# Wider sums of exponentials, a query transpose on VectorE, and one transfer on another queue in a clustered-attention and feed-forward kernel

## The chip, the cores and the metric

The kernel runs on one core of a Trainium2 chip. The metric is the device time of one launch in microseconds (us), the median of several runs. The engines of a core run their own instruction streams in order and meet at semaphores: PE (TensorE) multiplies, DVE (VectorE) and ACT (ScalarE) work on elements, POOL (GpSimd) here mostly issues transfers, SP (SyncE) issues transfers only.

## What is computed

Attention within clusters, for 4 batches of 8 heads with 768 positions of 64 features, and then a layer norm and a two-layer network on each position:

```python
q_assign = argmax(einsum('bhsd,hcd->bhsc', q_n, c_n))     # q_n, k_n, c_n: q, k, centroids at unit length
k_assign = argmax(einsum('bhsd,hcd->bhsc', k_n, c_n))     # 16 centroids per head
mask = q_assign[:, :, :, None] == k_assign[:, :, None, :]
scores = where(mask, q @ k.T / sqrt(64), -1e9)
attn = exp(scores - max);  attn = attn / (sum(attn) + 1e-9)
x = (attn @ v) laid out as (batch, 768, 512)
xn = (x - mean) / sqrt(var + 1e-6) * g_ln
out = x + relu(xn @ w_ch1) @ w_ch2                        # w_ch1 512x2048, w_ch2 2048x512
```

All inputs are 4-byte floats but the two weight matrices, which come as 8-byte floats and are turned into 4-byte floats on the chip.

## The kernel before

**Pairs, slots, steps.** Two heads are handled together, so that they fill 128 partitions; there are 16 such pairs, n = 0 to 15. A pair is cut in two slots (halves of 384 queries, `g`), a slot in six steps of 128 keys (`c`). A step has three parts in `scores`: two bf16 matmuls that put the cluster mask into a PSUM tile (three such tiles exist), two 4-byte matmuls that add q·k (L407), and one exponential of 128x768 elements on ACT (L402) into a tile `e`, of which there are eight. `weigh` multiplies `e` by v (L419) and, on DVE, adds it to the running sum of exponentials `es` (L433 for the first two, L436 for each later one), so that a slot has five adds of 768 columns. `finish` divides by those sums for an earlier pair: part 0 is a matmul with ones (`den`, L456), part 1 a reciprocal (L471) and transfers that spread it, part 2 a product (L489, L493), part 3 a transpose and a store (L501, L504).

**Preparing the next pair.** During pair n the kernel prepares pair n+1. `prep_transpose` turns k and q so that the features lie on partitions. It has two ways. If the load wrote 32x32 blocks in the right places (`load_blocks`, L86, runs of 128 bytes), one DVE transpose of 128x768 completes the job (L281). Otherwise the load is a plain one (L113), PE does six transposes into PSUM (L286), and ACT copies them out (L291). The set `blocks` holds which: k for all pairs from 1 on, q only for pair 1 and pairs 8 to 15. Then come the similarities to the centroids (`prep_sims`, PE), their transposes (`prep_turn`, PE), the nearest centroid (`prep_route`, DVE, L338 and L340) and the mask (`prep_onehot`, `prep_mask`, PE and ACT).

**Weights.** The 8-byte weights come in 32 chunks of 128x512. `load_weight` fetches one (L237, 512 KB, issued by SP) into the tile `raw`. `split_weight` (L246, L249, L252) reads the upper words of `raw`, `join_weight` (L261, L265, L266) reads its lower words last of all and sends the sum on by a transfer. During attention one such tile exists, `bufs=limit[1]` with

```python
    limit = [NWC, 1]
```

so the load of the next chunk can start only when L266 of the last one has ended. `convert` gives a chunk to both slots of pairs 0 to 6 and to the first slot of pairs 7 to 14, 22 chunks in all; the other ten are converted during the first batch's network.

**Order.** Inside attention the order of PE, DVE, ACT and POOL is the order in which the code is written (`manual_schedule`); SP is placed by the scheduler. In each slot the code writes: the transposes of pair n+1 (first slot only), six `scores`, preparation, six `weigh` with their adds, `finish` parts 1, 2, 3 (second slot), split, join, the next `load_weight`, and in the first slot `load(n+1, "v")`, `prep_turn` and `prep_route`.

**After attention.** The network works through four batches in seven-product block form (`product`, L774; `second_product`, L867).

Of the kernel before, what the change touches and what calls it, by code (L numbers as in the profile page):

```python
# [19 lines left out]
def kernel(  # L20
# [49 lines left out]
    def ps(name, dt=F32, n=512):  # L70
# [4 lines left out]

    TWICE = 7

    blocks = {
        (n, name) for n in range(1, len(pairs)) for name in ("qk" if n == 1 or n > TWICE else "k")
    }  # L80

    def load_blocks(n, name):
        b, pr = pairs[n]
# [10 lines left out]
    def load(n, names):  # L94
        if n >= len(pairs):
            return
        b, pr = pairs[n]
        for name in names:

            if (n, name) in blocks:  # L100
                load_blocks(n, name)
                continue
            shape = [P, 2, NT, D] if name == "v" else [P, NT, 2, D]
            t = loads.tile(
                shape, F32, tag=name, name=f"{name}_sb", bufs=2 if name == "v" else 1
            )

            parts = 1 if n or name == "v" else NHALF
            for g in range(parts):
                cs = slice(g * NT // parts, (g + 1) * NT // parts)  # L110
                for j in range(2):
                    queue = nc.scalar if parts > 1 and j else nc.sync
                    queue.dma_start(  # L113
                        out=t[:, j] if name == "v" else t[:, cs, j, :],
                        in_={"q": q, "k": k, "v": v}[name][b, 2 * pr + j].rearrange(
                            "(p c) d -> p c d", p=P
                        )[:, cs, :],
                    )
            loaded[n][name] = t
# [1 line left out]
    load(0, "q")  # L121

    c_sb = const.tile([H * NCL, D], F32, name="c_sb")
    nc.gpsimd.dma_start(out=c_sb, in_=centroids.rearrange("h c d -> (h c) d"))
    load(0, "k")

    ident = const.tile([P, P], F32, name="ident")
# [1 line left out]
    identb = const.tile([P, P], BF16, name="identb")  # L129
    nc.gpsimd.tensor_copy(identb, ident)  # L130

    once = attn.tile([P, 2, HC], F32, tag="e", name="once", bufs=8)
    zeros = once[:, 0, : P // 2].bitcast(BF16)
    nc.vector.memset(zeros, 0.0)
    ones = const.tile([P, Q], F32, name="ones")
# [135 lines left out]

    prepared = {n: {} for n in range(len(pairs))}

    def prep_transpose(n, side, halves=range(NHALF)):
        src = loaded[n]["qk"[side]]
        if 0 in halves:
            prepared[n][side] = heads.tile([P, S], F32, tag=f"t{side}", name=f"t{side}")
        t_sb = prepared[n][side]
        if (n, "qk"[side]) in blocks:
            if 0 in halves:  # L280
                nc.vector.transpose(t_sb, src)  # L281
            return
        if n:
            t = ps_s.tile([P, 2, 512], F32, tag="s", name="qk_ps")
            for c in range(NT):
                nc.tensor.transpose(  # L286
                    t[:, c // TH, c % TH * P : (c % TH + 1) * P],
                    src[:, c, :, :].rearrange("p h d -> p (h d)"),
                    ident,
                )  # L290
            nc.scalar.copy(t_sb.rearrange("p (g c) -> p g c", g=NHALF), t[:, :, :HC])  # L291
            return
        for g in halves:
            t = ps_s.tile([P, 2, 512], F32, tag="s", name="qk_ps")[:, 0]
            for c in range(TH):
                nc.tensor.transpose(
                    t[:, c * P : (c + 1) * P],
                    src[:, g * TH + c, :, :].rearrange("p h d -> p (h d)"),
                    ident,
                )  # L300
            if side == 0 or g == 1:
                nc.scalar.copy(t_sb[:, g * HC : (g + 1) * HC], t[:, :HC])
            else:
                nc.vector.tensor_copy(t_sb[:, g * HC : (g + 1) * HC], t[:, :HC])
# [86 lines left out]
    def scores(i, first="mask", parts=("mask", "qk", "exp")):  # L391
        n, g, c = steps[i]
        st = prepared[n]
        if parts[0] == first:
            st["s", i] = ps_s.tile([P, 2, 512], F32, tag="s", name="s_ps")
        s = st["s", i]
        keys, cols = slice(c * P, (c + 1) * P), slice(g * HC, (g + 1) * HC)
        rows = [slice(j * D, (j + 1) * D) for j in range(2)]
        for part in parts:
            if part == "exp":  # L400
                e = attn.tile([P, 2, HC], F32, tag="e", name="e", bufs=8)
                nc.scalar.activation(e, s[:, :, :HC], AF.Exp, scale=SCALE)  # L402
                soft[i] = e
                continue
            for j in range(2):
                of_keys, of_queries = st["m"][j] if part == "mask" else [st[i][rows[j]] for i in (1, 0)]
                nc.tensor.matmul(  # L407
                    s[:, j, :HC], of_keys[:, keys], of_queries[:, cols],
                    start=part == first, stop=part != first, skip_group_check=True,
                )  # L410

    def weigh(i):
        n, g, c = steps[i]
        e = soft[i]
        if c == 0:
            accs[n, g] = ps_a.tile([P, 512], F32, tag="a", name="a_ps")
        acc = accs[n, g]
        for j in range(2):
            nc.tensor.matmul(  # L419
                acc[j * D : (j + 1) * D, :HC],  # L420
                loaded[n]["v"][:, j, c, :],
                e[:, j, :],
                start=(c == 0),
                stop=(c == NT - 1),
            )

        if c == 1:
            if n + 1 < len(pairs):
                es = last.tile([P, 2, HC], F32, tag="es", name="es", bufs=3)
            else:  # L430
                es = xpool.tile([P, 2, HC], F32, tag="row", name="es", bufs=2)
            sums[n, g] = es
            nc.vector.tensor_tensor(es, soft.pop(i - 1), soft.pop(i), ALU.add)  # L433
        elif c > 1:
            es = sums[n, g]
            nc.vector.tensor_tensor(es, es, soft.pop(i), ALU.add)  # L436
        if c == NT - 1:
            if g == 0:
                if n + 1 < len(pairs):
                    xs[n] = last.tile([P, S], F32, tag="x", name="x", bufs=3)  # L440
                else:

                    late["all"] = xpool.tile([P, 3, S], F32, tag="sums", name="late", bufs=2)
                    xs[n] = late["all"][:, 0]
            nc.scalar.copy(xs[n][:, g * HC : (g + 1) * HC], accs.pop((n, g))[:, :HC])  # L445

# [229 lines left out]
    with tc.manual_schedule(engines=order | {mybir.EngineType.Pool}):  # L678
        for u in range(len(pairs) * slots):
            n, slot = divmod(u, slots)  # L680
            nxt = n + 1 < len(pairs)
            own = range(GROUP * u, GROUP * (u + 1))
            if slot == 0 and not nxt:
                finish(n - 1, 0)
            if slot == 0 and nxt:
                for side in (1, 0):
                    if (n + 1, "qk"[side]) in blocks:
                        prep_transpose(n + 1, side)
                        load(n + 2, "qk"[side])
            for i in own:  # L690
                if i >= AHEAD:
                    scores(i)
            if slot == 0:
                if n and nxt:
                    finish(n - 1, 0)
                if nxt:
                    prep_sims(n + 1)
            elif nxt:
                prep_onehot(n + 1)
                prep_mask(n + 1, 0)  # L700
                prep_mask(n + 1, 1)
                if n + 2 < len(pairs) and (n + 2, "q") not in blocks:
                    prep_transpose(n + 2, 0)
                    load(n + 3, "q")
            for job in extra.pop((n, f"between {slot}"), ()):
                job()
            for i in own:
                weigh(i)
            if slot and nxt:
                if n:  # L710
                    finish(n - 1, 1)
                if n > 1:
                    finish(n - 2, 2)
                    finish(n - 2, 3)
            if (n, slot) in convert:
                m = convert[n, slot]
                split_weight(m)
                join_weight(m)
                load_weight(m + 1)
            if slot == 0:  # L720
                load(n + 1, "v")
                if nxt:
                    prep_turn(n + 1)
                    prep_route(n + 1)
                else:
                    for part in (2, 3):
                        finish(n - 2, part)
                    finish(n - 1, 1)
            elif not nxt:
                for part in (2, 3):  # L730
                    finish(n - 1, part)
            for job in extra.pop((n, slot), ()):
                job()
# [472 lines left out]
```

## Time and profile before

| | |
|---|---|
| time, median of 3 runs | 933.51 us (930.01 to 934.81) |
| span of the profiled execution | 929.1 us |
| busy, share of the span: PE, DVE, ACT, POOL | 99%, 66%, 38%, 8% |
| attention, pairs 0 to 15 | about the first 343 us |
| DVE busy in attention, for example 110 to 160 us | 46.87 of 50 us |
| the same in the last 289 us | 120.45 of 289 us |

The page of a profile gives for each engine the time in which it worked, then groups of equal instructions with count and mean duration, then the transfers. The trace behind it can be asked for instructions in order of time (the timeline), for waits, and for busy time in stretches. Starts of consecutive instructions are what counts for a rate: the durations shown overlap a little, or leave a short gap where the next one needs the result. The whole-run share of an engine hides stages: DVE is at 66% over the run, but at 94% in parts of attention.

### The profile page before, as it was taken

What the parts mean: (1) busy time and instruction counts of PE and PEld (TensorE: products, weight loads), DVE (VectorE), ACT (ScalarE), POOL (GpSimd) and SP (SyncE); (2) the same over time, 40 slices, a digit from 0 to 9 for tenths busy, and PEclk for the clock granted to TensorE, in tenths of its full rate; (3) what the DMA queues carried; (4) which work ended last, traced back from release to release, by engine and by line L of the source; (5) the groups of instructions that cost most, each with busy time, mean ns of one, the idle gap of its engine ahead of it and who ended that gap; (6) DMA issues with size and microseconds to landing.
All of it is one profiled execution on the core that took longest, in us unless ns stands there. A gap on an engine that the chain in (4) does not pass through costs nothing.

```text
span 929.1 us, 12604 instructions
## 1 busy us (share of the span) xinstructions
PE 918.7 (99%) x4670; PEld 589.1 (63%) x4670; DVE 614.6 (66%) x1104; ACT 349.8 (38%) x551; POOL 78.3 (8%) x146
## 2 busy tenths in 40 slices
PE   8999999999999999999999999999999999999997
PEld 5444444444444445568886558886557887556886
DVE  4988999999899978889772436472346372434331
ACT  4677777767777653330003331002331001332000
POOL 2121222211211112110000000000000000000000
PEclk9999999999999999999999999999999999999999
DMA  7576888999888455645530002120002021000011
GB/s 153 128 162 125 183 177 166 210 185 166 175 175 162 100 119 142 159 91 170 176 112 8 1 0 94 55 74 17 1 0 86 18 96 40 0 1 6 30 46 37
DMA packets 177061, 89.35 MB, mean 96 GB/s; under 512 B 144096, under 2 KB 160592, under 8 KB 176992
## 3 DMA queue, kind: packets, MB, share of 16 engines
q1 hardware_dynamic: 167648, 73.06, 32.8%
q0 software_dynamic: 7744, 15.02, 8.1%
q8 instruction: 39, 0.64, 0.3%
q10 hardware_dynamic: 1600, 0.39, 0.2%
q14 instruction: 30, 0.25, 0.1%
HBM read 62.52 MB, written 17.52 MB: 86 GB/s over the span
## 4 chain that ended last, share of the span: by engine, by line
PE 92%; DVE 3%; DMA 3%; issue 1%; SPq 1%; ACT 0%; DVEq 0%; ACTq 0%
PE x_ps L867 18%; PE x_ps L774 18%; PE s_ps L407 13%; PE a_ps L419 12%; PE z_ps L867 9%; PE z_ps L774 9%; PE y_ps L867 4%; PE y_ps L774 4%; PE den_ps L456 1%; DMA v_sb<-in_v_dram 1%; PE sim_ps L313 1%; DVE es L436 1%; DMA raw<-in_moe_w_ch_dram 1%; PE simT_ps L329 1%; PE oh_ps L355 1%
## 5 line engine op out<-in xcount | busy, mean ns | idle before, releaser
L402 ACT ACTIVATE e<-s_ps 128x768 f32<-128x768 f32 x192 | 151.6, 811 | 24.3 <-PE s_ps L407 21.8
L407 PE MATMUL s_ps<-t,t 64*128 64x384 f32 x768 | 155.1, 483 | 0.0
L436 DVE TENSOR_TENSOR es<-es,e 128x768 f32<-128x768 f32 x128 | 122.7, 958 | 13.4
L419 PE MATMUL a_ps<-e,v_sb 128*64 128x384 f32 x768 | 130.9, 490 | 0.0
L419 PEld LDWEIGHTS a_ps<-e,v_sb 128*64 128x64 f32 x768 | 52.3, 137 | 70.0 <-issue 59.0
L794 DVE TENSOR_TENSOR h<-z_ps,u 128x384 f32<-128x384 f32 x64 | 35.6, 557 | 91.7 <-PE z_ps L774 69.2
L407 PEld LDWEIGHTS s_ps<-t,t 64*128 64x128 f32 x768 | 68.1, 188 | 35.0 <-issue 34.4
L867 PE MATMUL x_ps<-w2t,h 128*128 128x256 f32 x384 | 84.5, 379 | 0.0
L802 ACT ACTIVATE h<-h 128x384 f32<-128x384 f32 x96 | 49.5, 522 | 85.8 <-DVE h L794 85.8
L867 PEld LDWEIGHTS x_ps<-w2t,h 128*128 128x128 f32 x384 | 72.8, 190 | 10.1
L407 PE MATMUL s_ps<-m,mask 64*128 64x384 bf16 x192 | 62.1, 324 | 1.6 <-ACT e L402 1.2
L407 PE MATMUL s_ps<-mask,m 64*128 64x384 bf16 x192 | 62.0, 324 | 0.4 <-DVE mask L378 0.4
L789 ACT COPY u<-x_ps 128x384 f32<-128x384 f32 x64 | 30.6, 478 | 75.1 <-PE x_ps L774 75.1
L878 DVE TENSOR_TENSOR o_sb<-x_ps,xb 128x256 f32<-128x256 f32 x48 | 20.2, 422 | 49.8 <-PE x_ps L867 49.8
L789 ACT COPY p<-x_ps 128x384 f32<-128x384 f32 x32 | 14.9, 467 | 97.4 <-PE x_ps L774 97.4
L774 PE MATMUL x_ps<-xn,w 128*128 128x384 f32 x128 | 46.6, 487 | 0.6 <-ACT late L445 0.6
L774 PE MATMUL x_ps<-xt,ws 128*128 128x384 f32 x128 | 46.6, 487 | 0.0
L774 PE MATMUL x_ps<-xt,w 128*128 128x384 f32 x128 | 46.5, 486 | 0.0
L774 PE MATMUL x_ps<-xn,ws 128*128 128x384 f32 x128 | 46.5, 486 | 0.0
L774 PE MATMUL z_ps<-xt,ws 128*128 128x384 f32 x128 | 46.5, 486 | 0.0
L774 PE MATMUL z_ps<-xn,ws 128*128 128x384 f32 x128 | 46.5, 486 | 0.0
L774 PE MATMUL y_ps<-xn,w 128*128 128x384 f32 x128 | 46.5, 486 | 0.0
(147 smaller groups left out, 1350.7 us busy)
## 6 DMA issues: line engine op xcount, KB each, us to landing
raw<-in_moe_w_ch_dram SPq DMA_DIRECT2D x32, 512.0 KB, 5.3
w<-tb POOLq DMA_DIRECT2D x32, 256.0 KB, 5.8
v_sb<-in_v_dram SPq DMA_DIRECT2D x32, 192.0 KB, 4.8
xr<-x_d SPq DMA_DIRECT2D x24, 256.0 KB, 2.8
xb<-x_d SPq DMA_DIRECT2D x48, 128.0 KB, 2.2
out_dram<-o_sb SPq DMA_DIRECT2D x48, 128.0 KB, 1.7
k_sb<-in_k_dram SPq DMA_DIRECT2D x62, 96.0 KB, 5.9
rb<-row POOLq DMA_DIRECT2D x30, 192.0 KB, 4.4
```

What stands on the lines that cost most here:

```text
L313: nc.tensor.matmul(sim[r : r + Q, :HC], cT[:, pr, :, :].rearrange("p j c -> p (j c)"), prepared[n][side][:, g * HC : (g + 1) * HC], start= ...
L329: nc.tensor.transpose(simT[:, c * P : (c + 1) * P], sim_sb[:, c * P : (c + 1) * P], ident)
L402: nc.scalar.activation(e, s[:, :, :HC], AF.Exp, scale=SCALE)
L407: nc.tensor.matmul(s[:, j, :HC], of_keys[:, keys], of_queries[:, cols], start=part == first, stop=part != first, skip_group_check=True,)
L419: nc.tensor.matmul(acc[j * D : (j + 1) * D, :HC], loaded[n]["v"][:, j, c, :], e[:, j, :], start=(c == 0), stop=(c == NT - 1),)
L436: nc.vector.tensor_tensor(es, es, soft.pop(i), ALU.add)
L774: nc.tensor.matmul(bank[:, :HC], lhs[:, c, :], rhs[:, c, :], start=first and c == 0, stop=c == NDH - 1, skip_group_check=True,)
L789: nc.scalar.copy(t, bank[:, :HC])
L794: nc.vector.tensor_tensor(h, bank[:, :HC], other, ALU.add)
L802: nc.scalar.activation(h, h, AF.Relu)
L867: nc.tensor.matmul(bank[:, :MH], hidden[lhs + (c,)][:, tt * P : (tt + 1) * P], rhs[:, c, :], start=first and c == 0, stop=c == NFH - 1, sk ...
L878: nc.vector.tensor_tensor(o, bank[:, :MH], x, ALU.add)
```

## The change

It has four parts, and is for taking work from PE and ACT and making fewer, wider DVE instructions.

1. Exponentials of two steps share one tile of 128x(2x768); four such tiles take the place of eight. The sums move from `weigh` to a new `add_up`, after the six `weigh` of a slot: part 0 adds the first two tiles in one instruction of 1536 columns, part 1 adds the third in another and then folds the two halves in one of 768. The last pair keeps five adds of 768.
2. q of pairs 2 to 7 is loaded in blocks and turned by DVE like the others; the PE transposes and ACT copies of these pairs go.
3. The order within a slot: `finish` parts 2 and 3 come first, then `split_weight`, then `weigh`, the wide adds with the reciprocal between them, and `join_weight` with the next `load_weight` last.
4. The centroids are fetched by SP, between the first loads of q and k, and not by POOL.

```diff
-    blocks = {
-        (n, name) for n in range(1, len(pairs)) for name in ("qk" if n == 1 or n > TWICE else "k")
-    }
...
-            if (n, name) in blocks:
+            if n and name != "v":
                 load_blocks(n, name)
...
-    nc.gpsimd.dma_start(out=c_sb, in_=centroids.rearrange("h c d -> (h c) d"))
+    nc.sync.dma_start(out=c_sb, in_=centroids.rearrange("h c d -> (h c) d"))
...
-                e = attn.tile([P, 2, HC], F32, tag="e", name="e", bufs=8)
+                if c % 2 == 0:
+                    soft[i // 2] = attn.tile([P, 2, 2, HC], F32, tag="e", name="e", bufs=4)
+                e = soft[i // 2][:, c % 2]
...
-            nc.vector.tensor_tensor(es, soft.pop(i - 1), soft.pop(i), ALU.add)
-        elif c > 1:
-            es = sums[n, g]
-            nc.vector.tensor_tensor(es, es, soft.pop(i), ALU.add)
...
+    def add_up(n, g, parts=range(2)):
...
+        if 0 in parts:
+            two = xpool.tile([P, 3, S], F32, tag="sums", name="two", bufs=2)
+            two = two[:, :2].rearrange("p h (j c) -> p h j c", j=2)
+            sums[n, g] = two
+            nc.vector.tensor_tensor(two, soft.pop(u), soft.pop(u + 1), ALU.add)
+        if 1 in parts:
+            two = sums[n, g]
+            nc.vector.tensor_tensor(two, two, soft.pop(u + 2), ALU.add)
+            es = last.tile([P, 2, HC], F32, tag="es", name="es", bufs=3)
+            nc.vector.tensor_tensor(es, two[:, 0], two[:, 1], ALU.add)
+            sums[n, g] = es
...
-                if n + 2 < len(pairs) and (n + 2, "q") not in blocks:
-                    prep_transpose(n + 2, 0)
-                    load(n + 3, "q")
             for job in extra.pop((n, f"between {slot}"), ()):
                 job()
+            if slot and n > 1 and nxt:
+                finish(n - 2, 2)
+                finish(n - 2, 3)
+            m = convert.get((n, slot))
+            if m is not None:
+                split_weight(m)
             for i in own:
                 weigh(i)
-            if slot and nxt:
-                if n:
-                    finish(n - 1, 1)
-                if n > 1:
-                    finish(n - 2, 2)
-                    finish(n - 2, 3)
-            if (n, slot) in convert:
-                m = convert[n, slot]
-                split_weight(m)
+            add_up(n, slot, (0,))
+            if slot and n and nxt:
+                finish(n - 1, 1)
+            if nxt:
+                add_up(n, slot, (1,))
+            if m is not None:
                 join_weight(m)
                 load_weight(m + 1)
```

## The prediction

> **What bounds the kernel now.** I read the page's busy shares first, then the busy time by pair, then the order of DVE and SP inside one pair, then how long the weight chunks take to land.
>
> The busy shares say PE. The chain of waits says so too for the network (PE x_ps, z_ps and y_ps lines), but in attention DVE must be read beside it. Each of these lines is one pair (start:end, length, then busy time of PE, PEld, DVE, ACT, POOL with instruction counts, clock, share of the DMA engines, GB/s):
>
> ```profile
> 66.00:87.00 21.00, 21.00 (x153) 10.20 (x155) 17.34 (x26) 15.27 (x21) 4.62 (x7) 1.00 0.71 155
> 108.00:129.00 21.00, 21.00 (x153) 10.20 (x153) 19.82 (x31) 15.18 (x20) 4.74 (x7) 1.00 0.83 171
> 150.00:171.00 21.00, 20.45 (x147) 9.44 (x147) 19.82 (x31) 14.38 (x19) 4.71 (x7) 1.00 0.82 183
> 171.00:191.30 20.30, 20.30 (x147) 9.56 (x147) 19.17 (x29) 14.38 (x19) 3.65 (x6) 1.00 1.03 198
> ```
>
> ```profile
> 86.96 4.95 PE s_ps L407 x36
> 93.01 4.02 PE a_ps L419 x24
> ...
> 107.93 3.03 PE s_ps L407 x23
> 110.96 4.91 DMA v_sb<-in_v_dram
> ...
> 152.82 5.05 DMA v_sb<-in_v_dram
> ```
>
> The second view is the chain of waits by time (start, length, what). Second-slot scores start at 86.96 and again at 107.93: a pair takes 20.97 us. Between the scores ending at 91.91 and the weighing at 93.01 lie 1.10 us, where the mask transposes and the six q transposes stand; later pairs without q on PE have 0.44 us there (175.88 to 176.32) and take 20.3 us (170.93, 191.25, 211.56). So PE is full, q costs it 0.66 us a pair, and DVE has about one microsecond of slack.
>
> How thin that slack is shows in the DVE timeline across a slot border:
>
> ```profile
> 78.36 0.69 DVE L266 SCALAR_TENSOR_TENSOR tb<-raw,tb 128x512 f32<-128x512 uint32 x1
> 78.97 0.97 DVE L281 STREAM_TRANSPOSE t<-k_sb 128x768 f32<-128x768 f32 x1
> 79.87 0.92 DVE L433 TENSOR_TENSOR es<-e 128x768 f32<-128x768 f32 x1
> 80.89 4.15 DVE L436 TENSOR_TENSOR es<-es,e 128x768 f32<-128x768 f32 x4
> 86.31 0.43 DVE L246 TENSOR_SCALAR ta<-raw 128x512 uint32<-128x512 uint32 x1 [1.27 <-DMA raw<-in_moe_w_ch_dram]
> 86.77 0.69 DVE L249 SCALAR_TENSOR_TENSOR ta<-raw,ta 128x512 uint32<-128x512 uint32 x1
> 87.38 0.42 DVE L252 TENSOR_SCALAR tb<-raw 128x512 uint32<-128x512 uint32 x1
> 87.84 0.69 DVE L261 SCALAR_TENSOR_TENSOR w<-tb,ta 128x512 f32<-128x512 uint32 x1
> 88.56 0.45 DVE L265 TENSOR_SCALAR tb<-w 128x512 uint32<-128x512 uint32 x1
> 89.05 0.69 DVE L266 SCALAR_TENSOR_TENSOR tb<-raw,tb 128x512 f32<-128x512 uint32 x1
> 89.66 0.55 DVE L338 TENSOR_REDUCE best<-simT_ps 128x24 f32<-128x384 f32 x1
> ```
>
> ```profile
> 79.08 0.35 SPq L237 DMA_DIRECT2D raw<-in_moe_w_ch_dram  x1
> 89.77 0.36 SPq L237 DMA_DIRECT2D raw<-in_moe_w_ch_dram  x1
> ```
>
> ```profile
> DMA to landing us min/median/max: 4.2/5.6/7.2
> ```
>
> The reader is to see a ring. L266, the last reader of `raw`, ends; 0.1 us later SP issues the next chunk (79.08, 89.77); it lands 4.2 to 7.2 us after issue (last fence: the loads issued between 20 and 172 us); only then can L246 run. At present one transpose and five adds stand in that gap, 6 us or more of useful work, and even so DVE waited 1.27 us at 86.31.
>
> **What the Trainium skill says.** "VectorE: DVE Perf Modes", section "The TRN2 errata", gives (N+151)/0.96 ns for a 4-byte tensor_tensor add: 957 ns for N = 768, and L436 has a mean of 958 ns, so it agrees; for N = 1536 it makes 1757 ns, which no row shows yet. "DMA: Bandwidth & Descriptors", "Rules for kernel authors", says to issue a transfer early, compute, and wait late; the ring above is how the kernel does that now. "Perfetto Trace Analysis", "Sequencer Loop" and "Identifying the Most-Contended Engine", says that an engine's instruction waits in its queue for its semaphores, and that matmul busy time is no measure of distance from the limit; the stretches above agree in so far as PE's 21.00 of 21.00 does not show that DVE is nearly as full.
>
> **The change part by part.**
> *Adds.* Start to start, an add of 768 that needs the one before it takes 1.04 us (4 in 4.15). A wide one should take 1.76 + 0.08 = 1.84 us. A slot goes from 0.92 to 1.06 for the first plus 4 x 1.04, about 5.2 us, to 1.84 + 1.84 + 1.04 = 4.72 us: 0.5 us less, 0.95 us a pair on DVE. If width brought nothing it would be 5.2, if the fixed part were larger 4.9; both ends matter little below.
> *q.* Pairs 2 to 7: PE loses 6 x 0.66 = 4.0 us, ACT six copies of 0.80 us, which were hidden. DVE gets one transpose a pair, 0.94 us (L281 on q). Net DVE load: nothing won. The q loads become runs of 128 bytes (3,072 packets a pair), issued behind those of k: SP needs up to 7.13 us for k and 4.3 to 5.0 us for q (165.21, 172.44, 134.99). That ends about 13 us after the border, just before the next chunk has to be issued; I price it at nothing, with a risk upward.
> *Double tiles.* Four of two steps hold what eight of one did. A slot fills three, so the next may run two steps ahead; its third exponential needs the first wide add of the slot before. That add stands ten microseconds before its successor; nothing is lost.
> *Centroids on SP.* DVE waits for them until 4.86 us, but the similarities at 8.39 us also need k, whose copy out of PSUM ends at 7.8 us. At most half a microsecond either way; counted as nothing.
> *Order.* This carries the forecast. The three split instructions now stand ahead of the adds, and join behind them. Split reads `raw`; nothing lies between one join and the next split but the transposes (2 x 0.93 = 1.9 us, first slot) or routing, product and output transpose (1.2 + 1.9 = 3.0 us, second slot). There is one `raw` tile. DVE must therefore stand at L246 till the chunk lands, and the adds, the join, `prep_route` and the transposes queue behind it. PE waits for these: exponentials for a free tile, the mask for `prep_route`, the similarities for the transposes. Split is 1.53 us (86.31 to 87.84), join 1.80 us (87.84 to 89.66).
>
> Time from the end of one join to the end of the next: 0.1 issue + landing + 1.53 + 4.72 + 1.80 = 8.15 us + landing, and 0.14 us more in a second slot (reciprocal): 8.29. Landing: chunks issued at the end of a second slot took 4.3, 7.2, 5.6, 5.7 and 6.2 us (issued 36.7, 79.1, 101.2, 121.9, 142.7), mean 5.8, with the k loads behind them. Those issued in a first slot: 4.2 us is the only one listed (46.0); the v loads that follow such chunks at once took 4.91 and 5.05 us (the DMA lines of the chain above), so I take 4.6. A pair becomes 8.29 + 4.6 + 8.15 + 5.8 = 26.8 us against 20.97 us.
>
> Chunk 0: transposes from 16.79, split at 18.6 (chunk landed at 17.8), join done at 18.6 + 1.53 + 4.72 + 1.80 = 26.65 us. Then 13 rounds, seven ending in a second slot and six in a first: 7 x 12.89 + 6 x 13.95 = 173.9, so the join of chunk 13 (end of pair 6) ends at 200.6 us. Before, it ended at 163.7 us, where the transposes start. That is +36.9 us. In pair 7 one more round: its routing is done 13.95 + 1.2 = 15.1 us after that point, while PE would ask for it after 12.15 us (7.2 to its second-slot scores, 4.95 for these): +3 us. From pair 7 on there is one chunk per pair, landed long before, and PE sets 20.3 us as now. The 4.0 us that PE saves lie in pairs that DVE now sets, and bring nothing. The network is as before. Sum: +39.9, 933.5 + 39.9 = 973.
>
> **The rivals.**
> A, PE stays the bound and only its saving shows: 933.5 - 4.0 = 929.5 us, faster. For it: fewer, wider DVE instructions, and chunks that could land early. Against: even the shortest landing, 4.2 us, leaves 8.2 + 4.2 = 12.4 us a slot, above PE's 10.2.
> B, the wait is filled but DVE is the bound: its load of about 20.97 us a pair neither falls nor rises (-0.95 + 0.94), so the PE saving brings nothing: 933 to 934 us. Against: it needs a second `raw` tile, and there is none.
> C, same ring, slower landings, since q blocks now share the DMA engines (share 1.03 in the stretch after 171 us where both q and k come in blocks): 7.2 us every time makes 7 x 15.49 + 6 x 15.35 = 200.5, join of chunk 13 at 227.2, +63.5, and +4.4 in pair 7: 1001 us. The other end, 4.2 us each time, gives 7 x 12.49 + 6 x 12.35 = 161.5, +24.5 and +1.4: 959 us.
>
> **How the numbers follow.** The ring with landings near those seen: 0.84, 973 us. C: 0.08. B: 0.03. A: 0.05. The range 957 to 993 holds the ring from 4.2 us landings to about 6.6 us on average, and leaves out most of C, B and A. Slower takes the first two, 0.92; same 0.03; faster 0.05.
>
> **What would show it.** In the profile after: L243 (split's first) waiting for DMA raw at every slot of pairs 1 to 6, some 4 us in first slots (5.9 - 1.9) and 1.7 us in second ones (4.7 - 3.0), 40 us in all; pairs of about 27 us until some 200 us and 20.3 us after; wide adds of 1.76 us; PE idle for about 40 us there; the network unchanged in length. Pairs 0 to 6 at 20.3 us, or a wait at L243 of a few us in all, would make it wrong; a wait of over 6 us each would mean C.

## The result and the profile after

| | before | after |
|---|---|---|
| median | 933.95 us (930.01 to 936.96, 6 runs) | 960.51 us (958.76 to 963.5, 6 runs) |
| span of the profiled execution | 929.1 us | 957.5 us |
| ratio after to before | | 1.0291, 95% interval 1.026 to 1.0323 |

The change makes the kernel 2.9% slower. The busy times hardly moved: DVE 610.4 us against 614.6, PE 923.3 against 918.7. The time is in waits: PE is idle for 34.2 us of the span, against 10.4 us before. Nearly all of it is in pairs 0 to 7: the second-slot scores of pair 8 start at 219.28 us against 191.25 us, 28.0 us later, and the spans differ by 28.4 us (the medians by 26.6 us).

Busy time after, by stretches near one pair long (columns as before):

```profile
80.00:105.00 25.00, 20.90 (x151) 9.48 (x145) 19.63 (x26) 14.45 (x19) 4.54 (x7) 1.00 0.66 128
105.00:130.90 25.90, 23.00 (x148) 10.09 (x145) 19.78 (x27) 14.42 (x19) 4.60 (x7) 0.93 0.72 141
130.90:156.80 25.90, 21.97 (x153) 10.06 (x153) 20.66 (x28) 14.65 (x20) 4.52 (x7) 1.00 0.72 143
209.00:229.50 20.50, 20.50 (x149) 9.62 (x147) 20.03 (x26) 14.45 (x19) 3.84 (x7) 1.00 1.00 209
229.50:250.00 20.50, 20.50 (x151) 9.76 (x149) 19.65 (x28) 14.47 (x20) 3.86 (x6) 1.00 0.97 190
```

Where two chunks are converted in a pair, neither PE nor DVE is full, and the share of the DMA engines is lower than it was (0.72 against 0.83 in a like stretch): no engine is at its limit, so a chain of waits must set the time. From 209 us on PE is full again.

The chain of waits after, from one chunk to the next (start, length, what), shows it ("..." marks lines left out, here as in all fences and code):

```profile
112.59 4.98 DMA raw<-in_moe_w_ch_dram
...
117.59 0.44 DVE ta L243
...
118.05 0.69 DVE ta L246
118.74 0.34 DVE tb L249
119.08 1.68 DVE two L436
...
120.85 1.77 DVE two L439
...
122.64 0.96 DVE es L441
123.60 0.61 DVE w L258
...
124.24 0.44 DVE tb L262
124.70 0.70 DVE tb L263
125.42 5.29 DMA raw<-in_moe_w_ch_dram
```

Load, split, two wide adds and the fold, join, load: 12.83 us for one slot, with no PE and no ACT in it. Before, the chain of waits ran through PE's scores and weighing up to 111 us; from there to about 165 us it ran through DVE and transfers, with one landing of `raw` among them (142.70 us, 6.21 us long). So the kernel before was already close to this ring. DVE's own view of the same border, with the wait named at the end of the line:

```profile
111.87 0.69 DVE L263 SCALAR_TENSOR_TENSOR tb<-raw,tb 128x512 f32<-128x512 uint32 x1
112.48 0.97 DVE L275 STREAM_TRANSPOSE t<-k_sb 128x768 f32<-128x768 f32 x1
113.37 0.94 DVE L275 STREAM_TRANSPOSE t<-q_sb 128x768 f32<-128x768 f32 x1
117.59 0.43 DVE L243 TENSOR_SCALAR ta<-raw 128x512 uint32<-128x512 uint32 x1 [3.28 <-DMA raw<-in_moe_w_ch_dram]
```

The waits of 15 to 200 us (waiter, releaser, us in total, times, longest):

```profile
DVE ta L243 <- DMA raw<-in_moe_w_ch_dram: 37.9, 14, 4.3
PE sim_ps L297 <- DVE t L275: 17.2, 7, 2.7
PE oh_ps L339 <- DVE onehot L324: 5.2, 5, 1.4
```

Before, DVE waited for `raw` for 1.6 us in two places. PE shows the same loss at second hand: it waits for DVE's transposes and for the routing, which queue behind L243.

### The profile page after: what moved, and what is told of

Read it like the earlier page. It is cut to its first block, busy times and chain, and to the rows that moved or that the text cites. A ratio compares the mean times of both kernels' runs of the same rounds, so it can differ in the third digit from the quotient of the medians.

```text
span 957.5 us, 12287 instructions
## 1 busy us (share of the span) xinstructions
PE 923.3 (96%) x4634; PEld 586.5 (61%) x4634; DVE 610.4 (64%) x1050; ACT 345.9 (36%) x545; POOL 77.4 (8%) x145
## 4 chain that ended last, share of the span: by engine, by line
PE 80%; DVE 11%; DMA 7%; SPq 1%; issue 0%; ACT 0%; DVEq 0%; ACTq 0%
PE x_ps L863 17%; PE x_ps L770 17%; PE z_ps L863 9%; PE s_ps L392 9%; PE z_ps L770 9%; PE a_ps L404 8%; DMA raw<-in_moe_w_ch_dram 7%; PE y_ps L863 4%; PE y_ps L770 4%; DVE two L439 3%; DVE two L436 2%; DVE es L441 1%; DVE tb L263 1%; DVE ta L246 1%; DVE w L258 1%; PE den_ps L453 1%
## 5 line engine op out<-in xcount | busy, mean ns | idle before, releaser
L404 PE MATMUL a_ps<-e,v_sb 128*64 128x384 f32 x768 | 134.9, 502 | 0.0
L392 PEld LDWEIGHTS s_ps<-t,t 64*128 64x128 f32 x768 | 68.1, 188 | 34.9 <-issue 34.2
L436 DVE TENSOR_TENSOR two<-e 128x1536 f32<-128x1536 f32 x30 | 52.5, 1750 | 8.7 <-ACT e L388 8.7
L439 DVE TENSOR_TENSOR two<-two,e 128x1536 f32<-128x1536 f32 x30 | 52.8, 1758 | 1.7
```

The source lines that it names most:

```text
L392: nc.tensor.matmul(s[:, j, :HC], of_keys[:, keys], of_queries[:, cols], start=part == first, stop=part != first, skip_group_check=True,)
L404: nc.tensor.matmul(acc[j * D : (j + 1) * D, :HC], loaded[n]["v"][:, j, c, :], e[:, j, :], start=(c == 0), stop=(c == NT - 1),)
L436: nc.vector.tensor_tensor(two, soft.pop(u), soft.pop(u + 1), ALU.add)
L439: nc.vector.tensor_tensor(two, two, soft.pop(u + 2), ALU.add)
```

## The experiments

The ring of the prediction says: there is one `raw` tile, and with split ahead of the adds too little useful work stands between a chunk's request and its first use. Two rivals could also slow pairs 2 to 7: DVE overloaded by the q transposes (with the 128-byte q loads), or exponentials held up by double tiles that a wide add frees late.

| version | median us | ratio to before (95% interval) |
|---|---|---|
| split moved back | 926.4 | 0.9953 (0.9934 to 0.9971) |
| kernel before, new place of split alone | 992.58 | 1.0664 (1.0641 to 1.0687) |
| kernel before, q on DVE alone | 933.01 | 1.0014 (1.0004 to 1.0025) |
| kernel before, double tiles and wide adds alone | 932.12 | 1.0009 (1.0001 to 1.0017) |
| changed, two `raw` tiles | 927.78 | 0.9943 (0.9923 to 0.9963) |
| changed, product and stores put late | 984.23 | 1.0534 (1.0504 to 1.0564) |
| split moved back, centroids by POOL | 927.27 | 0.9939 (0.9922 to 0.9956) |
| split moved back and two `raw` tiles | 927.68 | 0.9943 (0.9922 to 0.9965) |
| kernel before, wide adds and q on DVE | 931.66 | 0.9995 (0.9982 to 1.0008) |

The first four shared one set of runs of the kernel before (931.62 us), the next four another (933.21 us), the last a third (932.26 us).

**Split moved back**

```diff
-            m = convert.get((n, slot))
-            if m is not None:
-                split_weight(m)
             for i in own:
                 weigh(i)
...
+            m = convert.get((n, slot))
             if m is not None:
+                split_weight(m)
                 join_weight(m)
```

> The changed kernel with the three split instructions moved back to stand right before join, behind the adds; all else as changed. Ring theory (one raw tile, and split ahead of the adds, so that DVE stands still while each chunk lands): the adds and transposes stand in the gap again, 1.8 + 4.5 = 6.3 us or more, the wait at split's first instruction falls from 38 us to under 8, and the time is 929 to 935 us; DVE then has about 20.7 us of work a pair against PE's 20.3. Rival, DVE load (q transposes and 128-byte q loads): the split's place does not matter, 950 us or more. Rival, double tiles (exponentials wait for a tile that the wide add frees late): 950 us or more.

926.4 us, below the range given: PE sets 20.3 us a pair, and DVE's work fits in that after all. The wait for `raw` is 0.8 us in two places, and PE is full:

```profile
87.00:108.00 21.00, 21.00 (x153) 10.02 (x151) 20.48 (x29) 15.13 (x21) 4.47 (x8) 1.00 0.87 174
108.00:129.00 21.00, 21.00 (x153) 10.00 (x151) 19.70 (x27) 15.13 (x21) 4.93 (x8) 1.00 0.91 173
150.00:171.00 21.00, 21.00 (x153) 9.69 (x150) 20.48 (x28) 15.12 (x21) 4.62 (x7) 1.00 0.97 206
```

Three lines of code, with all else as changed, are worth some 32 us (1.0291 - 0.9953 of 933 us). Both rivals fall: the q transposes, the q loads and the double tiles are all still in this version.

**The place of split alone, on the kernel before**

```diff
+            m = convert.get((n, slot))
+            if m is not None:
+                split_weight(m)
             for i in own:
                 weigh(i)
...
-            if (n, slot) in convert:
-                m = convert[n, slot]
-                split_weight(m)
+            if m is not None:
                 join_weight(m)
```

> The kernel before with one edit: split stands ahead of the six weigh, join stays where it is. Ring theory: a round is 0.1 + landing + 1.4 + 5.2 + 1.8 us, plus 2.0 in second slots where the three finish parts stand inside the ring here, so about 14 us to first and 15 us to second slots, 13 rounds: 980 to 992 us, slower than the whole change. Rivals (DVE load, double tiles): 933 us, since neither is in it.

992.58 us, just above the range given. The wait for `raw` is 56.2 us in 12 places. The loss is larger than in the whole change. Here the product and the output transpose stand between split and join, inside the ring, while in the changed kernel they fill part of the wait; the version with product and stores put late, below, shows what this alone is worth. The five narrow adds, longer than the wide ones, stand in the ring too.

**The q transposes alone, and the wide adds alone**

```diff
-        (n, name) for n in range(1, len(pairs)) for name in ("qk" if n == 1 or n > TWICE else "k")
+        (n, name) for n in range(1, len(pairs)) for name in "qk"
```

> The kernel before with q of pairs 2 to 7 loaded in blocks and turned by DVE; nothing else. Ring theory: no ring, but DVE gains 0.9 us a pair on about 21.0 and becomes the bound at 21.5 to 21.9 us while PE falls to 20.3: 933 to 939 us. DVE-load theory: most of the 26.6 us of the change appear here, 950 us or more.

```diff
-        if c == 1:
...
-            nc.vector.tensor_tensor(es, es, soft.pop(i), ALU.add)
...
             for i in own:
                 weigh(i)
+            add_up(n, slot)
```

> The kernel before with double tiles and the wide adds after the six weigh; split, join, finish and the q transposes as before. Ring theory: DVE loses 1.2 us a pair, PE is the bound at 20.97 us, 931 to 935 us. Double-tile theory: exponentials wait for tiles, 945 us or more.

(The double tiles and the rest of `add_up` are as in the change.) 933.01 and 932.12 us: neither gains anything, and neither costs anything near the 2.9%. In the first, DVE sets the time, in a stretch where PE has lost its q transposes and a pair still takes as long:

```profile
108.00:129.00 21.00, 19.90 (x145) 9.24 (x143) 19.82 (x30) 14.38 (x19) 4.74 (x7) 1.00 0.83 169
129.00:150.00 21.00, 19.90 (x143) 9.04 (x140) 19.85 (x29) 13.91 (x19) 4.60 (x7) 1.00 0.83 169
```

PE works 19.90 of 21.00 us. DVE's durations add up to only 19.8 us, and yet it has no room: from 85 to 150 us its trace shows no wait at all, and its pairs of transposes start 21.6 us apart (121.58 and 143.18 us). The rest is in the short gaps between instructions that need each other's result: four adds with a mean of 0.96 us take 4.15 us. The kernel before is as full: DVE has 19.82 us of durations between 108 and 129 us, and from 85 to 171 us it waits only 1.27 and 0.29 us.

In the second it is the other way round: DVE has more room, and PE is at its 21 us for most pairs. In the last two PE waits (18.97 of 21.00 us busy from 150 to 171 us). The chunks make DVE wait 6.0 us in four places here; the adds that stand in the gap are shorter, and three of the landings are long (6.6, 7.2 and 7.5 us). These runs do not separate the two.

**A second `raw` tile, split left where the change put it**

```diff
-            es = last.tile([P, 2, HC], F32, tag="es", name="es", bufs=3)
+            es = last.tile([P, 2, HC], F32, tag="es", name="es", bufs=2)
...
-    limit[0] = len(convert)
+    limit[:] = len(convert), 2
...
         load_weight(0)
+        load_weight(1)
...
-                load_weight(m + 1)
+                load_weight(m + 2)
```

(and one `xr` tile less, with its rows loaded one step ahead)

> The changed kernel with a second raw tile, so that chunk m+2 is loaded when chunk m is joined; room for it comes from one es tile and one xr tile less (rows loaded one step ahead, not two). The order stays: split ahead of the adds. Ring theory: what costs is that only one tile exists, so the wait at split falls from 38 us to under 3 and the time to 925 to 933 us. A rival, that split's place ahead of the adds costs in itself (for example by delaying the tiles of the exponentials): 940 us or more with hardly any wait for raw.

927.78 us, and no wait of DVE for `raw` is left between 15 and 200 us. So split's place does not cost in itself; it costs together with the single tile. Both cures at once:

> Both cures together: split moved back, and two raw tiles. If the ring alone is the loss, one cure is enough and this is within 2 us of the version with split moved back (926.4 us), since PE sets 20.3 us a pair there already. If some ring wait still counts there, it is faster by more.

927.68 us: one cure is enough.

**Why the chunks landed sooner than forecast**

```diff
-            if slot and n > 1 and nxt:
-                finish(n - 2, 2)
-                finish(n - 2, 3)
...
             if nxt:
                 add_up(n, slot, (1,))
+            if slot and n > 1 and nxt:
+                finish(n - 2, 2)
+                finish(n - 2, 3)
```

> The changed kernel with finish parts 2 and 3 (product, output transpose and its four stores) put back behind the adds, ahead of join, so that the stores of y are issued just before the chunk of the next first slot, as in the kernel before. If these stores are what made such chunks land in 5.8 us before and in 4.5 us after, the landing goes back to 5.3 us or more, and with 1.9 us moved into the ring in five pairs the time is 972 to 980 us. If the landing has to do with something else, it stays at 4.5 us and the time is 968 to 971 us.

984.23 us, above the upper forecast. SP's own timeline shows why in two lines, and the chain of waits has the landings of the chunks issued at the end of second slots, first in this version:

```profile
89.99 3.08 SPq L501 DMA_DIRECT2D x_d<-y  x4
93.19 0.45 SPq L234 DMA_DIRECT2D raw<-in_moe_w_ch_dram  x1
```

```profile
93.19 6.57 DMA raw<-in_moe_w_ch_dram
...
123.11 5.73 DMA raw<-in_moe_w_ch_dram
...
152.23 8.40 DMA raw<-in_moe_w_ch_dram
...
184.04 6.97 DMA raw<-in_moe_w_ch_dram
```

and then in the changed kernel:

```profile
38.61 4.22 DMA raw<-in_moe_w_ch_dram
...
62.80 4.39 DMA raw<-in_moe_w_ch_dram
...
87.33 4.52 DMA raw<-in_moe_w_ch_dram
...
138.57 4.32 DMA raw<-in_moe_w_ch_dram
...
163.63 4.57 DMA raw<-in_moe_w_ch_dram
```

With the four stores of y just ahead of it, a chunk takes 5.7 to 8.4 us to land, against 4.2 to 5.0 us in the changed kernel. (The two such chunks that this version issues before its first store of y took 4.4 and 5.4 us.) The chunk is also issued later: L263 ends at 91.72 us, but SP is still issuing stores until 93.07. My expectation left out this second delay, some 1.5 us a pair, and most landings are well above its 5.3 us.

**The centroids, and whether the new order is needed**

> The version with split moved back, and the centroids fetched by POOL again. My working gave this part nothing, at most half a microsecond: 926 to 927 us, the first second-slot scores at 23.7 to 24.1 us. If the SP fetch is worth more: 928 us or more, and those scores later than 24.5 us.

927.27 us, just above the 926 to 927 given, and the scores start at 23.77 us (23.70 with the fetch by SP): the SP fetch has no effect that these runs can tell.

> The kernel before with the double tiles and wide adds, and with q of all later pairs turned by DVE; the order of finish, split and join, and the centroids, as before. Alone, neither brought anything (932.1 and 933.0 us). If the two need each other (the adds free the 0.9 us of DVE that the q transpose takes, and PE falls from 20.97 to 20.3 us a pair), this is 926 to 929 us, and the new order is of no use at all. If the gain of the version with split moved back came from its order of finish, this stays at 931 to 934 us.

931.66 us: no gain, so the second of the two cases came, and the two parts together do not suffice. This version differs from the one above only in that `finish` parts 2 and 3 stand behind the adds and the reciprocal does not stand between them, and it loses some 4 us to it. DVE in this version, across a second slot:

```profile
89.42 0.08 DVE L340 DVE_READ_ACCUMULATOR onehot<-simT_ps,best 128x1 f32 x1
89.95 1.76 DVE L454 TENSOR_TENSOR two<-e 128x1536 f32<-128x1536 f32 x1 [0.45 <-ACT e L404]
```

and the same place with split moved back (centroids by SP):

```profile
87.03 0.08 DVE L324 DVE_READ_ACCUMULATOR onehot<-simT_ps,best 128x1 f32 x1
87.03 0.95 DVE L490 TENSOR_TENSOR xn<-x,rb 128x768 f32<-128x768 f32 x1
88.02 0.98 DVE L498 STREAM_TRANSPOSE y<-xn 128x768 f32<-128x768 f32 x1
88.92 1.72 DVE L436 TENSOR_TENSOR two<-e 128x1536 f32<-128x1536 f32 x1
```

A wide add needs four exponentials before it can start. If it comes first, DVE waits for ACT (7.5 us in nine places between 15 and 200 us, against 2.7 us in three in the version above, which in turn waits for `raw` for 3.6 us against 1.3). If product and transpose of an older pair come first, the exponentials are mostly ready. That the 4 us come from this wait is read from the traces, not shown by a run; the reciprocal's place, which differs too, was not tried alone. So the change's new order was half right: moving `finish` is what lets the other parts pay, and moving split forward undid it.

The version with split moved back is faster than both kernels, though by only 0.5% of the kernel before (0.9953, 926.4 us).

## Why the prediction was right

It forecast 973 us, in 957 to 993; measured are 960.51 us. Direction and mechanism hold step by step. The measured time lies 12.5 us below the forecast, near the lower end of the range, mainly through one term.

- *The order carries the forecast, through one `raw` tile.* This is shown from both sides: the loss is cured by moving split back or by a second tile, and it is brought about in the kernel before by split's place alone.
- *The waits at L243.* Forecast were 40 us in all, some 4 us in first slots and 1.7 us in second ones; measured are 37.9 us, 2.5 to 3.3 us in the first slots of pairs 1 to 6 and 1.5 to 3.3 us in the second ones (mostly 2.1). That the sum agrees so well is in part luck, since the two errors partly cancel. PE's idle time rose by 23.8 us, where about 40 us were forecast.
- *Rounds.* Forecast were joins ending at 26.65 us (chunk 0) and 200.6 us (chunk 13). The instructions that follow them start at 26.4 us (the routing after chunk 0) and 188.83 us (the transposes after chunk 13). A round took 12.5 us on average, not 13.4. Three terms differ:
  - *Landing at the end of second slots: 5.8 us assumed, 4.5 us measured* (the six chunks issued from 38.6 to 163.6 us), 6 x 1.3 = 7.8 us. This is the mis-sized term. I took it from five loads of the kernel before. Just ahead of four of them the stores of y had been issued (5.6 to 7.2 us); the fifth had none ahead of it and took 4.3 us. The change moves these stores to the start of DVE's work in the slot, and I read that in the diff without drawing the conclusion. Putting them back brought 5.7 to 8.4 us.
  - *Split, adds and join: 8.05 us assumed, 7.72 us measured* in a first slot (42.85 to 50.57). A second slot takes the same 7.72 us (104.76 to 112.48), 0.46 us less than assumed there, since the reciprocal hides between the adds. Together this is 5 us. Neighbours that do not need each other's result overlap: the add starts 0.33 us after split's last instruction has started, which itself lasts 0.42 us (105.83, 106.16).
  - *Landing at the end of first slots: 4.6 us assumed, 4.8 us measured,* which takes some 1.2 us back.
- *Pair 7: +3 us.* At the scores of pair 8 the changed kernel is 28.0 us late, at the end of chunk 13 it was 25.1 us late: 2.9 us.
- *Adds of 1.76 us.* L436 has a mean of 1750 ns and L439 of 1758 ns, so the formula of the Trainium skill, "VectorE: DVE Perf Modes", section "The TRN2 errata" (1757 ns), holds at 1536 columns.
- *The PE saving is buried.* Right in the changed kernel. Freed of the ring it shows: 926.4 us, by the ratio 4.4 us less than the kernel before (2.7 to 6.1 us by its interval), against the 4.0 us of rival A.
- *Rival B was wrong in its premise,* that DVE stays the bound once the wait is filled. With product and transpose ahead of the adds, DVE fits in 20.3 us a pair. With the old order, in the version with wide adds and q on DVE, about B's 933 us is what came (931.66).
- *That PE is full and DVE has about one microsecond of slack* was half right. That microsecond is mostly the gaps between dependent instructions; from 85 to 171 us DVE was about as full as PE in the kernel before. The forecast did not rest on this. Nor do the stretches shown there tell how far PE is from its own limit, which is what the cited page on traces is about.
- *The centroids, the double tiles and the q loads were priced at nothing.* No run shows a cost of any of them.

## What to carry to other kernels

A load into a single buffer makes a ring: last read, request, landing, first read. What stands between the first and the last read lengthens the ring, and only what stands between the last read and the next first read hides the landing. Moving a reader forward in program order can turn a hidden transfer into the bound though no engine gets more work. Price a landing as it will be in the changed kernel: look at what is queued just ahead of it there, not in the trace at hand. And when instructions are merged into wider ones, look for the work that should fill the longer wait for their inputs.

## What the runs showed of the hardware that was not expected

The granted clock of PE, the part of its full clock rate that the trace shows as given, is lower in some stretches in which PE waits again and again: 0.93 in the stretch from 105 us shown above, and 0.76 in the kernel before with split's place alone, in a stretch where PE works 13.54 of 21.00 us:

```profile
129.00:150.00 21.00, 13.54 (x81) 6.91 (x81) 13.10 (x20) 8.98 (x12) 1.46 (x2) 0.76 0.52 98
```

In others with much waiting it stays at 1.00: from 80 and from 130.90 us in the changed kernel, and from 150 to 171 us in the run with 0.76, where PE works 16.63 of 21.00 us. In the changed kernel the weighing that starts at 115.15 us takes 5.73 us, against 4.09 us for the one at 126.95. So PE's busy time can rise while it has less to do: it went from 918.7 to 923.3 us, though 36 transposes are gone. The longer weighing is hidden there, since the chain of waits has no PE in it. The runs do not show what triggers the lower clock.
